# A gated-MLP layer behind a state-space convolution: where the output weights are queued, the order of the first loads, the order of four f tiles, and the second pair's first weights

## The chip, the cores and the metric

The kernel runs on one core of a Trainium2 chip. The core has a matrix engine (TensorE, PE in the profile, with its weight loads as PEld), a vector engine (VectorE, DVE), a scalar engine (ScalarE, ACT), GpSimd (POOL), and SyncE (SP), which here only issues transfers. Sixteen DMA engines move data between the device memory and the on-chip memory; SP, ACT and POOL each have a queue of their own into them. The metric is the device time of one execution in microseconds. The median of three runs of the kernel before is 1020.4 us (1020.36 to 1022.5).

## The reference

One layer of a network, 2048 tokens of width 640, in float32. Cut to what matters:

```python
mod = (silu(c) @ w_mod).reshape(6, 640)          # sa, ca, ga, sb, cb, gb
h = layernorm(x) * (1 + ca) + sa
x = x + ga * ssm_conv(h)                         # long convolution, by transforms over 2048 tokens
h = layernorm(x) * (1 + cb) + sb
gate = h @ w1; up = h @ w3                       # [2048, 640] @ [640, 1728]
out = x + gb * ((silu(gate) * up) @ w2)          # [2048, 1728] @ [1728, 640]
```

## The kernel before

The first 427 us compute the modulation and the convolution up to its last inverse transform and leave the transformed rows in `zs` in device memory. The change lies in what follows, the second layer norm and the gated MLP.

**Tiling.** The 2048 tokens are four quarters of 512, taken in two pairs: quarters A and B of pair 0, then of pair 1. The 1728 columns of w1 and w3 are cut into 14 f tiles of 128 (`NFT`); the last one, 13, holds the 64 remaining columns of both. float32 operands are split into a rounded high part and a low part (`split`, L1025: ACT copies the high part `gh` or `uh`, DVE subtracts to get the low part `gl` or `ul`), and a product is three matmuls, high x high, high x low, low x high (`prod3`, L1046).

**Stages of a pair.** First the quarters' input: a tile of 128 tokens gets its `zs` rows (`x_get`, L941: five transfers of z and one of x on SP's queue), its last transform on PE, the addition and the statistics on DVE, the root on POOL (`x_mid`, L950), the normalization on ACT (`x_norm`, L965), and is then turned by transposes on PE (`turn_a`, `turn_b`). Pair 0 has its first four tiles from before (`x_first`, L913); the next four are done between the first f tiles. For pair 1 all of it is done between the output steps of pair 0 (`prepare`, L1255, a table of step numbers).

Then the f tiles. Some are done plainly (`plain`, L1058: quarter A or B alone, 15 matmuls for the gate and 15 for the up part): 0, 13, 1 and 2 in pair 0, 13 alone in pair 1. The others go through `seven` (L1113), a Strassen-Winograd scheme over both quarters with sums of weight blocks made on POOL (`w_sums`) and split (`w_split`). Its operands `T1`, `T2`, `T4` and `T3` are sums of the turned inputs (`x_sums`, `x_sum_split`, `x_late`).

Then the outputs (`outputs`, L1173), 28 steps of 15 matmuls for a pair: 14 f tiles for quarter A, then 14 for B. Step n issues the load of the w2 tile of step n + 3 (`load`), has POOL multiply that of n + 2 by gb (`gate`), has ACT and DVE split that of n + 1 together with h (`operands`), runs `side(n)`, and then the matmuls. At the end of a quarter DVE adds the accumulators to x, and `tail` turns and adds the last 128 columns.

**What sets the order.** All weights share one ring of four buffers, `rw` (L1038). A scheduler orders the instructions of each engine, except where `in_order` holds: then an engine's instructions stay in the order of the program. This holds for the output stage. An engine's queue of transfers is in order too: a transfer that waits for its buffer holds all those behind it. `issue_after` puts an instruction behind another on its engine.

The lines that matter for the steps below:

```python
            load(n + 3)                                   # L1211, in the loop over output steps
            gate(n + 2)
            operands(n + 1)
            got = [x_get(4 + i, x, there, nc.scalar if i == 1 else SQ) ...]   # L1303
        for f in simple:                                  # L1318
            hB[f] = h_tile()
            plain("B", f, hB[f])
```

## Time and profile before

| | |
|---|---|
| median of three runs | 1020.4 us |
| the profiled execution | 1021.97 us |
| its span | 1020.2 us |
| mean granted clock of TensorE | 0.937 |
| HBM read, written | 108.93 MB, 31.46 MB |

| engine | busy us | share of the span | instructions |
|---|---|---|---|
| PEld | 693.6 | 68% | 8214 |
| DVE | 721.7 | 71% | 1230 |
| ACT | 542.9 | 53% | 796 |
| POOL | 346.6 | 34% | 330 |

Rows of a timeline give the start in us from the span's start, the duration in us, the engine (SPq or ACTq is an engine issuing a transfer), the line, the operation with out<-in by the program's names, the count of merged instructions, and in brackets how long the engine had been idle and what released it. L102 is a helper that records every operation of this part of the program, so groups are told apart by their tiles: `gh<-rw` is the cast of a weight's high part, `gl<-rw,gh` the subtraction for its low part, `A<-zs` a z load, `T<-...` a normalized tile or, as `T<-s`, one of the sums' splits, `ident` marks a transpose, `rw<-rw,gbr` the multiply by gb, `S<-rw` a sum of weight blocks. Matmul rows name the moving operand first. The profiled time is taken on one execution; it is 1.77 us longer than its span.

### The profile page before, as it was taken

To read this page: it belongs to the slowest core of one execution; us is meant where nothing else is said; L and a number is where in the kernel's file an instruction comes from. 1 tells how busy PE (TensorE), PEld (TensorE's weight loads), DVE (VectorE), ACT (ScalarE), POOL (GpSimd) and SP (SyncE) were. 2 spreads that over 40 slices of the span, in tenths; PEclk is the share of its full clock that TensorE was granted. 3 is DMA by queue.
4 is the path that set the end of the run, shared out by engine and by line. 5 is a ranking of instruction groups with operands and counts; after the bars stand their busy time and mean duration, and the time that the engine had idled before them with its cause. 6 is when DMAs were issued, how large, how long until landed. Compare 5 with 4: busy or idle time off the path is not lost.

```text
span 1020.2 us, 20715 instructions
## 1 busy us (share of the span) xinstructions
PE 930.7 (91%) x8214; PEld 693.6 (68%) x8214; DVE 721.7 (71%) x1230; ACT 542.9 (53%) x796; POOL 346.6 (34%) x330
## 2 busy tenths in 40 slices
PE   5998798899889888788999999999889999999998
PEld 2535454666666666566888888766668888888876
DVE  4598966888888985657566675777586666676755
ACT  3658674999999954155433332354543333333332
POOL 1543332444454611313322231544352222233441
PEclk9855787999999999798999999999889999999999
DMA  9463495465555688593311112879432111113443
GB/s 260 167 236 116 189 210 175 124 162 141 142 147 145 179 214 262 177 251 96 91 52 52 52 53 93 220 241 235 129 117 78 52 52 52 52 39 91 129 158 126
DMA packets 104004, 141.73 MB, mean 139 GB/s; under 512 B 20612, under 2 KB 62724, under 8 KB 103908
## 3 DMA queue, kind: packets, MB, share of 16 engines
q1 hardware_dynamic: 98740, 129.66, 43.9%
q0 software_dynamic: 2304, 7.74, 2.4%
q10 hardware_dynamic: 2864, 3.02, 1.1%
q8 instruction: 64, 1.05, 0.4%
q14 instruction: 32, 0.26, 0.1%
HBM read 108.93 MB, written 31.46 MB: 138 GB/s over the span
## 4 chain that ended last, share of the span: by engine, by line
PE 59%; ACT 15%; DVE 9%; DMA 8%; issue 4%; POOL 4%; SPq 1%; ACTq 0%; DVEq 0%; POOLq 0%
PE ps L102 44%; ACT cs L135 3%; ACT A L135 3%; ACT ph L135 3%; DMA A<-zs 2%; PE pa L432 2%; PE p L570 2%; ACT L135 2%; DMA zs<-zt 2%; PE pq L444 2%; DMA rw<-in_w_dram 1%; PE pt L539 1%; PE pk L521 1%; PE pu L406 1%; PE pm L299 1%
## 5 line engine op out<-in xcount | busy, mean ns | idle before, releaser
L102 DVE TENSOR_TENSOR s<-ps,s 128x512 f32<-128x512 f32 x138 | 94.7, 687 | 77.6 <-PE ps L102 77.0
L472 POOL TENSOR_TENSOR ph<-thi,iota 128x1024 int32<-128x1024 int32 x40 | 85.4, 2134 | 177.2 <-DVE A L508 80.5
L102 DVE TENSOR_TENSOR gl<-rw,gh 128x640 fp32r<-128x640 f32 x89 | 84.3, 948 | 74.7 <-ACT gh L102 73.6
L102 ACT CAST gh<-rw 128x640 fp32r<-128x640 f32 x89 | 64.6, 726 | 122.6 <-POOL rw L102 66.6
L102 POOL TENSOR_TENSOR rw<-rw,gbr 128x512 f32<-128x512 f32 x56 | 82.6, 1483 | 123.1 <-DMA rw<-in_w_dram 117.9
L102 POOL TENSOR_TENSOR S<-rw 128x256 f32<-128x256 f32 x46 | 35.4, 771 | 178.0 <-DVE S0l L102 152.5
L102 PE MATMUL ps<-xA,gh 128*128 128x512 f32 x280 | 89.7, 399 | 2.8 <-ACT gh L102 2.2
L570 PE MATMUL p<-uk,s 128*64 128x256 f32 x640 | 79.3, 390 | 13.7 <-PE pa L432 5.6
L102 PE MATMUL ps<-gh,uh 128*128 128x512 f32 x224 | 88.2, 394 | 0.0
L102 PE MATMUL ps<-gl,uh 128*128 128x512 f32 x224 | 87.8, 392 | 0.0
L102 PE MATMUL ps<-gh,ul 128*128 128x512 f32 x208 | 81.6, 392 | 0.0
L570 PEld LDWEIGHTS p<-uk,s 128*64 128x64 f32 x640 | 45.3, 139 | 39.1 <-PE pa L432 8.4
L102 PEld LDWEIGHTS ps<-xA,gh 128*128 128x128 f32 x280 | 53.4, 192 | 15.9 <-ACT gh L102 3.5
L102 PE MATMUL ps<-xA,gl 128*128 128x512 f32 x140 | 55.3, 395 | 0.1
L135 ACT ACTIVATE A<-pa 128x1024 f32<-128x1024 f32 x40 | 40.4, 1023 | 25.7 <-PE pa L432 24.3
L497 DVE TENSOR_TENSOR E<-A,cs 128x1024 f32<-128x1024 f32 x40 | 50.3, 1257 | 1.7 <-ACT A L135 1.7
L504 DVE TENSOR_TENSOR A<-A,ph 128x1024 f32<-128x1024 f32 x40 | 50.1, 1253 | 0.0
L612 PE MATMUL pz<-Y,i 64*128 64x128 f32 x640 | 44.9, 284 | 4.5 <-issue 3.1
L102 PEld LDWEIGHTS ps<-gh,uh 128*128 128x128 f32 x224 | 42.5, 190 | 9.3 <-DVE xm L102 0.4
L102 PEld LDWEIGHTS ps<-gl,uh 128*128 128x128 f32 x224 | 42.5, 190 | 9.1
L612 PEld LDWEIGHTS pz<-Y,i 64*128 64x128 f32 x640 | 38.8, 188 | 14.3 <-issue 11.3
L539 PE MATMUL pt<-s,K 128*64 128x128 f32 x640 | 47.8, 293 | 0.5 <-ACT uk L138 0.5
(241 smaller groups left out, 2376.7 us busy)
## 6 DMA issues: line engine op xcount, KB each, us to landing
rw<-in_w_dram SPq DMA_DIRECT2D x52, 320.0 KB
rw<-in_wg_dram SPq DMA_DIRECT2D x33, 320.0 KB
us<-u SPq DMA_DIRECT2D x16, 640.0 KB
s<-in_s_dram SPq DMA_DIRECT2D x40, 256.0 KB
i<-in_i_dram SPq DMA_DIRECT2D x40, 256.0 KB
rw<-in_wu_dram SPq DMA_DIRECT2D x29, 320.0 KB
uk<-us SPq DMA_DIRECT2D x32, 256.0 KB
zs<-zt SPq DMA_DIRECT2D x32, 256.0 KB
```

The source lines that it names most:

```text
L102: ins = fn(*args, **kw)
L135: return tc.keep_in_program_order(S.activation(*args, **kw))
L299: PE.matmul(pm[g, :n], scb[:, k], w[:, k, :], start=(k < 4), stop=(k > 0), tile_position=(0, g.start))
L406: PE.matmul(pu[h][hh * 64:hh * 64 + 64, q, :320], s1r[r], x[r, hh * 320:hh * 320 + 320], start=not (one and h == 0), stop=True, tile_posit ...
L432: keep(PE.matmul(pA[s][:, rr, :], w[r, ch, :], r2[r, js, :].rearrange("p j b -> p (j b)"), start=st, stop=not st, tile_position=(r.start, 0)))
L444: keep(PE.matmul(pQ[s][:, rr, :256], w[r, ch, :], rv, start=(i == 0), stop=(i == 3), tile_position=(r.start, 0)))
L472: hold(G.tensor_tensor(p, bc(thi[:, sl], 2, NPH), bc(iota, 1, SD), op=OP.mult))
L497: keep(V.tensor_tensor(EC[s][:, :, 1:3, :], AA[s][:, :, 1:3, :], mid(cs[s]), op=OP.mult))
L504: keep(V.tensor_tensor(A[:, :, 1:3, :], A[:, :, 1:3, :], mid(ph[s]), op=OP.mult))
L539: keep(PE.matmul(pt[c * 64:c * 64 + 64, g, :], kk[:, g, :], s1[:, c, :], start=True, stop=True, tile_position=(0, c * 64)))
L570: keep(PE.matmul(p2[par * 64:par * 64 + 64, pi, c, :], s2[:, pi * 2 + par, c * 64:c * 64 + 64], uk[:, 0:kn + 1:kn, f, :], start=True, stop ...
L612: ins = keep(PE.matmul(pz[:, par, (g % 2) * 2 + pi, :], i1[r, pi, c, :], Y[r, pi, c, :], start=(c == 0), stop=(c == 1), tile_position=(par ...
```

## The change

Four things, all in the MLP part.

1. In `outputs`, the w2 loads of the loop go to ACT's queue instead of SP's (`load(n + 3, S)`), and stand behind `operands(n + 1)`. The first three loads of a pair stay on SP's.
2. At the start of pair 0, SP's transfers are kept in program order (`sp_order`), all z loads go on SP's queue, and the weights of f tiles 13 and 1 stand between them. The split of f tile 0's weights is traced ahead of `x_first`, that of 13 is held behind the last turned input. POOL's stores of x to `xs` are held behind the power of `x_first`.
3. The plain f tiles of quarter B run backwards (2, 1, 13, 0), and the split weights of the last tile of quarter A are used for the first of quarter B without a new load; in pair 1 this is f tile 13.
4. The first weights of pair 1 (13, then 0) are loaded at output steps 25 and 26 of pair 0 (`fetch`, `ahead`). The last `tail` of pair 0 runs after pair 1's plain tiles. In `prepare`, a step does normalizations first, then loads, turns, and `x_mid` last.

```diff
-        for i, n in enumerate((2, 5, 8, 9, 14, 15, 16, 17)):
+        mids = (6, 8, 11, 12, 17, 18, 19, 20)
+        for i, n in enumerate(mids):
+            at(n + 2, lambda i=i: x_norm(4 * q0 + i, got[i], tiles[i // 4]))
+        for i, n in enumerate((2, 5, 8, 9, 14, 15, 16, 17)):
...
+        for i, n in enumerate(mids):
+            at(n, lambda i=i: x_mid(4 * q0 + i, got[i], g))
+        at(25, lambda: fetch(NFT - 1, "wg"))
+        at(26, lambda: [fetch(0, n) for n in ("wg", "wu")])
...
-            load(n + 3)
+            operands(n + 1)
+            load(n + 3, S)
             gate(n + 2)
-            operands(n + 1)
...
+        side(n_all)
+        in_order[0] = False
+        yield
         for t in late:
             t()
-        side(n_all)
-        in_order[0] = False
...
-            got = [x_get(4 + i, x, there, nc.scalar if i == 1 else SQ) for i, (x, there) in enumerate(rooms)]
+            sp_order[0] = True
+            got = [x_get(4, x5[0], True)]
+            fetch(last_f, "wg")
+            got.append(x_get(5, x5[1], True))
+            fetch(1, "wg")
+            fetch(1, "wu")
+            got += [x_get(6, x_place("T40")), x_get(7, x_place("T20"))]
+            sp_order[0] = False
...
+            ws = ws or plain_weights(f, ends if pair == 0 and n == 1 else None)
+            end = plain("A", f, hA[f], ws, pair == 0)
+            if n < len(simple) - 1:
+                ws = None
...
-        for f in simple:
+        for n, f in enumerate(simple[::-1]):
             hB[f] = h_tile()
-            plain("B", f, hB[f])
+            ws = ws or plain_weights(f)
+            plain("B", f, hB[f], ws)
+            ws = None
```

On SP's queue, at the start of pair 0 (behind the convolution's last store of z), the rows of the difference; `A<-zs` is a z load, `T<-in_x` a load of x:

```order
-L102 DMA A<-zs 64x4x128 x10
-L102 DMA T_5417<-in_x_dram 128x640
-L102 DMA A<-zs 64x4x128 x5
-L102 DMA T_5418<-in_x_dram 128x640
+L102 DMA A<-zs 64x4x128 x5
+L102 DMA rw<-in_wg_dram 128x640
+L102 DMA A<-zs 64x4x128 x5
+L102 DMA rw<-in_wg_dram 128x640
+L102 DMA rw<-in_wu_dram 128x640
+L102 DMA A<-zs 64x4x128 x5
+L102 DMA T_5443<-in_x_dram 128x640
```

The three weights (13, then both of 1) stood behind all z loads and now stand behind five and ten of them; five z loads came over from ACT.

On ACT, between the casts of f tile 0's weights and the second x tiles, before:

```order
L102 CAST gh<-rw 128x640
L102 DMA A<-zs 64x4x128 x5
L102 CAST uh<-rw 128x640
L102 ACTIVATE T_5359<-xm,rs_5308 128x640
L102 ACTIVATE T_5363<-xm,rs_5308 128x640
```

and now, up to the first Silu behind the table load:

```order
L102 CAST gh<-rw 128x640
L102 CAST uh<-rw 128x640
L102 ACTIVATE T_5367<-xm,rs_5316 128x640
L102 ACTIVATE T_5371<-xm,rs_5316 128x640
L102 ACTIVATE xA_5381<-ps,modT 128x512
L102 ACTIVATE s_5390<-ps,modT 128x512
L102 ACTIVATE xA_5401<-ps,modT 128x512
L102 CAST xA_5392<-s_5390 128x512
L102 ACTIVATE s_5410<-ps,modT 128x512
L102 ACTIVATE xA_5421<-ps,modT 128x512
L102 CAST xA_5412<-s_5410 128x512
L102 CAST gh<-rw 128x640
```

The five issues are gone from between the two casts. The row that follows the last one is `CAST uh<-rw`, for f tile 1, and then the table load.

In the output stage of pair 0, on SP around output steps 15 to 18, before:

```order
L102 DMA out_dram<-xm 128x640 x4
L102 DMA rw<-in_w_dram 128x640
L102 DMA A<-zs 64x4x128 x5
L102 DMA xm<-in_x_dram 128x640
L102 DMA rw<-in_w_dram 128x640
L102 DMA A<-zs 64x4x128 x5
L102 DMA xm<-in_x_dram 128x640
L102 DMA rw<-in_w_dram 128x640
```

and on ACT at the same place now:

```order
L102 CAST gh<-rw 128x640
L102 CAST uh<-h 128x512
L102 DMA rw<-in_w_dram 128x640
L102 ACTIVATE s_7736<-ps,modT 128x512
L102 CAST xA_7738<-s_7736 128x512
L102 ACTIVATE s_7746<-ps,modT 128x512
L102 CAST xA_7748<-s_7746 128x512
L102 CAST gh<-rw 128x640
L102 CAST uh<-h 128x512
L102 DMA rw<-in_w_dram 128x640
```

The w2 loads stood on SP between the z and x loads and now stand on ACT behind the two casts of each step; SP keeps the z, x, xs and out transfers.

## Prediction before the run

> **What bounds the kernel now.** I read the page first, then the timeline of TensorE (PE) by the idle time in brackets, then the windows for the granted clock, and last the timelines of the engines named in the brackets.
>
> ```profile
> span 1020.2 us, 20715 instructions
> ...
> PE 930.7 (91%) x8214; PEld 693.6 (68%) x8214; DVE 721.7 (71%) x1230; ACT 542.9 (53%) x796; POOL 346.6 (34%) x330
> ...
> PEclk9855787999999999798999999999889999999999
> ...
> L102 DVE TENSOR_TENSOR gl<-rw,gh 128x640 fp32r<-128x640 f32 x89 | 84.3, 948 | 74.7 <-ACT gh L102 73.6
> ```
>
> PE is busy 91% of the span and bounds the kernel; of 40 slices three near the end of the convolution and the start of the two matrix stages fall under full clock; the last row, DVE's split of a weight (0.95 us on average), is used further down. The change touches nothing before about 427 us, so only PE's gaps behind that count:
>
> ```profile
> 434.71 2.45 PE L102 MATMUL ps<-ident,T 128*128 128x128 f32 x20 [2.37 <-ACT T L102]
> ...
> 444.84 1.52 PE L102 MATMUL ps<-A,i 64*32 64x256 f32 x32
> 448.55 0.73 PE L102 MATMUL ps<-xA,gh 128*128 128x512 f32 x2 [2.19 <-ACT gh L102]
> ...
> 463.96 0.33 PE L102 MATMUL ps<-ident,T 128*128 128x128 f32 x1 [2.62 <-ACT T L102]
> 466.01 2.18 PE L102 MATMUL ps<-ident,T 128*128 128x128 f32 x9 [1.71 <-ACT T L102]
> ...
> 677.21 0.47 PE L102 MATMUL ps<-uh,gh 128*128 128x512 f32 x1 [2.12 <-DVE xm L102]
> ...
> 705.66 0.87 PE L102 MATMUL ps<-A,i 64*32 64x384 f32 x14 [1.12 <-DVE xm L102]
> ...
> 722.54 1.33 PE L102 MATMUL ps<-ident,T 128*128 128x128 f32 x5 [4.63 <-ACT T L102]
> ...
> 740.41 0.51 PE L102 MATMUL ps<-uh,gl 128*128 128x512 f32 x1 [0.56 <-DVE gl L102]
> 742.08 0.50 PE L102 MATMUL ps<-ul,gh 128*128 128x512 f32 x1 [1.17 <-DVE ul L102]
> ...
> 752.40 1.22 PE L102 MATMUL ps<-xB,gh 128*128 128x512 f32 x2 [3.15 <-ACT gh L102]
> ```
>
> The columns are start, duration, line, operation, and in brackets the idle time before it with its releaser. They fall in three groups: the start of the first pair (2.37 + 2.19 + 2.62 + 1.71 = 8.89 us), the outputs of the first pair (2.12 + 1.12 + 4.63 + 0.56 + 1.17 = 9.60), and the start of the second pair (3.15). Three of them also cost clock. The windows give, after the bounds, the time, then busy time of PE, weight loads, DVE, ACT and POOL, then granted clock, DMA share and GB/s:
>
> ```profile
> 429.00:449.00 20.00, 14.86 (x99) 10.91 (x97) 9.15 (x21) 8.14 (x12) 3.19 (x6) 1.00 1.10 287
> ...
> 466.00:472.00 6.00, 5.99 (x19) 5.14 (x20) 4.32 (x6) 4.81 (x8) 1.28 (x1) 0.52 0.23 62
> ...
> 722.00:728.00 6.00, 5.46 (x16) 4.56 (x17) 3.80 (x4) 4.21 (x7) 1.30 (x1) 0.52 0.92 312
> ...
> 752.00:759.00 7.00, 6.58 (x16) 4.72 (x17) 4.97 (x12) 3.31 (x8) 0.00 (x0) 0.54 0.72 253
> 766.00:950.00 184.00, 184.00 (x814) 152.35 (x813) 122.18 (x191) 68.35 (x127) 51.73 (x57) 1.00 0.21 62
> ```
>
> Behind 466, 722 and 752 the clock is 0.52, 0.52 and 0.54; PE's busy time there loses 5.99 x 0.48 = 2.9, 5.46 x 0.48 = 2.6 and 6.58 x 0.46 = 3.0 us. From 766 to 950 PE is busy in all 184 us at full clock, 814 matmuls of 0.226 us each, and the second pair's outputs show no gap either: there nothing can be won, only lost. At most 8.9 + 9.6 + 3.2 + 8.5 = 30 us are there to be had.
>
> **Part 1: the first loads.** Three edits act here: five z loads leave ACT's queue for SP's, SP's list is pinned with the weights of f tiles 13 and 1 between the z loads, and POOL's four stores to xs come behind the power.
>
> ```profile
> 427.31 9.66 SPq L102 DMA_DIRECT2D A<-zs  x10
> ...
> 442.18 1.29 SPq L102 DMA_DIRECT2D rw<-in_wg_dram  x2
> ```
>
> ```profile
> 427.67 4.33 ACTq L654 DMA_DIRECT2D A<-zs  x5
> 432.04 0.73 ACT L102 CAST uh<-rw 128x640 fp32r<-128x640 f32 x1 [8.45 <-DMA A<-zs]
> 433.73 1.73 ACT L102 ACTIVATE T<-xm,rs 128x640 f32<-128x640 f32 x2 [0.97 <-DVE rs L102]
> ...
> 447.78 0.72 ACT L102 CAST gh<-rw 128x640 fp32r<-128x640 f32 x1 [7.30 <-DMA rw<-in_wg_dram]
> 448.52 1.28 ACT L102 ACT_TABLE_LOAD   x1
> 449.81 0.60 ACT L102 ACTIVATE s<-ps 128x512 f32<-128x512 f32 x1
> ...
> 465.03 0.92 ACT L102 ACTIVATE T<-T,nb,rs 128x640 f32<-128x640 f32 x1 [1.12 <-DVE nb L102]
> ```
>
> ```profile
> 429.97 0.42 DVE L102 BATCH_NORM_AGGREGATE mv<-st 128x2 f32<-128x30 f32 x2
> ...
> 450.44 0.69 DVE L102 TENSOR_TENSOR h<-ps,s 128x512 f32<-128x512 f32 x1 [1.08 <-ACT s L102]
> ```
>
> Before, ACT issued for 4.33 us and so cast uh at 432.04; DVE's ul stood behind that, and the normalization behind ul, at 433.73. Without the issues uh and ul are done while the statistics still run (they end at 429.97 + 0.42 = 430.4). POOL's add of 0.20 us and power of 1.05 us, no longer split by stores, then end at 431.8, and the normalization starts at 432.0: 1.7 us earlier. PE's transposes and f tile 0 move with it, and f tile 0 ends at 444.84 - 1.7 = 443.1.
>
> The larger piece is the next one. f tile 13's weight was issued at 442.18 and ACT had its cast at 447.78, 5.6 us later; table load, Silu and then DVE's h follow in line, h at 450.44. DVE's line from there to the last normalized tile (465.03, 14.6 us after h) is what holds PE until 466.01, and the changed kernel keeps that line nearly instruction for instruction. So the term is how far h moves. In the new list of SP ten z loads and three weights stand up to the last weight that ACT needs ahead of its table load. SP needed 9.66 us for ten z loads beside ACT's five; alone I put the fifteen over the same 9.66, so 0.64 each, and with 0.65 for a weight (1.29 for two) the list is out at 427.3 + 6.4 + 1.9 = 435.7. With the 5.6 us from issue to cast that the saturated DMA (share 1.10 from 429 to 449) gave before, its cast starts at 441.3, table load and Silu end at 443.9, and f tile 0's end at 443.1 plus Silu and issue allows 443.85. Thus h at 443.9 instead of 450.4: **6.5 us**. Bounds: if the weight lands only when everything has landed (449 by the window), h is at 451.5 and the term is -1; if the clock also stays up, 6.5 + 2.9 = 9.4.
>
> In the changed kernel PE is free for the transposes at 443.1 + 13.2 (two x_mid groups of 1.52, and 15 and 30 matmuls of f tiles 13 and 1, 3.4 and 6.8) = 456.3 and waits till 443.9 + 15.5 = 459.4, so about 3.1 us idle remain. The gap of 3.15 at 752.40 was enough to lower the clock, the gaps of 2.37 and 2.19 were not; I take the nearer one and count no clock here. [...]
>
> Running f tile 2 first for the second quarter spares a second load and split of its weights: work of ACT and DVE under a full PE, counted as nothing.
>
> **Part 2: output weights on ACT's queue.**
>
> ```profile
> 689.70 0.38 SPq L102 DMA_DIRECT2D rw<-in_w_dram  x1
> ...
> 694.14 0.38 SPq L102 DMA_DIRECT2D rw<-in_w_dram  x1
> 695.49 3.27 SPq L102 DMA_DIRECT2D A<-zs  x5
> ```
>
> ```profile
> 695.55 1.29 POOL L102 TENSOR_TENSOR rw<-rw,gbr 128x512 f32<-128x512 f32 x1 [5.23 <-DMA rw<-in_w_dram]
> ...
> 701.69 1.29 POOL L102 TENSOR_TENSOR rw<-rw,gbr 128x512 f32<-128x512 f32 x1 [3.47 <-DMA rw<-in_w_dram]
> ```
>
> ```profile
> 718.00:720.00 2.00, 0.00 (x0) 0.00 (x0) 2.00 (x1) 0.00 (x0) 2.00 (x2) 1.00 0.00 0
> ```
>
> The weights issued at 689.70 and 694.14 reached POOL's multiply at 695.55 and 701.69, 5.9 and 7.6 us later, each behind five z loads on the same queue. POOL's wait delays ACT's cast, DVE's split, then the x_mid work queued behind it, and in the end the normalized tile for which PE stops 4.63 us at 722.54; the DMA engines move nothing by then (the window from 718 to 720), so it is a chain of latencies. With the weight on ACT's own queue, issued behind uh of the tile after next, POOL gets it in time. From the last x_mid group at 705.66 to the transposes at 722.54 were 16.9 us; less the 5.9 us by which the weights ran late that is 11.0, and PE, with 15 matmuls or 3.4 us an iteration and 0.9 for x_mid, arrives after three iterations, 11.1 us. I count 5.5 of the 1.12 + 4.63, nothing of 2.12 (DVE's own line), nothing of 0.56 + 1.17 (POOL's x_sums, in the same order), and the clock's 2.6: **8.1 us**. Bounds 0 and 10.2 (with the 2.12). Cost: some 50 issues on ACT of 0.38 (SP's row) to 0.87 us (ACT's five z loads in 4.33). Two casts and an issue take 0.73 + 0.73 + 0.87 = 2.3 us of 3.4, so the issue is hidden by ACT's idle time; behind it stand normalizations and the next casts. Without that cover it would be 50 x 0.38 to 0.87 = 19 to 44 us. The wait for a free buffer is none: the buffer's last reader is DVE's split two iterations back.
>
> [...]
>
> **Part 3: the second pair's start.** f tile 13's weight is loaded ahead and serves both quarters.
>
> ```profile
> 745.67 1.89 POOL L102 TENSOR_TENSOR S<-rw 128x256 f32<-128x256 f32 x2
> ```
>
> ```profile
> 749.18 3.26 DVE L102 TENSOR_TENSOR xm<-ps,xm 128x512 f32<-128x512 f32 x8
> ...
> 757.27 0.42 DVE L102 TENSOR_TENSOR S1l<-S,S1h 128x256 fp32r<-128x256 f32 x1
> ```
>
> The 3.15 us at 752.40 are the wait for a second copy of that weight, cast by ACT just before; this load and cast no longer exist, and with them goes the clock's 3.0. POOL's weight sums, 745.67 before, find their weights loaded ahead and move up. Late next is DVE. PE, with the 30 matmuls of f tile 13's two quarters from 745.5 on and four transposes, asks for S1l at 752.9. DVE's line from its eight additions (749.18) to the end of S1l (757.7) took 8.5 us; the four of the additions that are 128 wide and not 512 (by size a quarter, 0.8) and an h (0.7) move behind S1l, which leaves 7.0 and 756.2. So S1l is 0 (if its line starts 3.3 us earlier, with POOL) to 3.3 us late; I take the middle, 1.6. 3.15 + 3.0 - 1.6 = **4.5 us**; bounds 0 (DVE's line decides all) and 6.2.
>
> **Sum.** 6.5 + 8.1 + 4.5 = 19.1. Where PE follows closer on DVE's splits I expect one more pair of small waits like those at 740.41 and 742.08, 1.7 us: 17.4. The profiled execution took 1021.97, which is 1.77 more than its span; it would become 1004.6. It lies 1.6 above the median of the runs, 1020.4, so the median becomes **1003.0**.
>
> **Rivals.**
> 1. Weights on ACT's queue land no earlier, since the DMA engines are shared: part 2 gives 0, 1020.4 - 9.3 = 1011.1. For it: a DMA share over 1 while the z loads run. Against: 5.9 and 7.6 us for a weight behind z loads, and idle DMA engines at the 4.63. [...]
> 2. The pinned list is too slow: ten z loads and three weights ahead of the Silu, part 1 gives about 0: 1009.5. For it: DMA saturated from 429 to 449, in which time 20 z loads, weights and stores must all pass.
> 3. The clock stays up at the first transposes and the 2.12 goes too: 1003.0 - 2.9 - 2.1 = 998.0.
> 4. Slower: a weight is now asked for only when ACT reaches its turn, not when its buffer is free. From issue to first use PE has three iterations (10.2 us) less the two casts ahead of the issue, multiply, cast and split (1.46 + 1.29 + 0.73 + 0.95 = 4.4): 5.8 us. With a landing of 7.6 (the row at 701.69) each third iteration of 28 stops PE 1.8 us, 17 us in all, and part 2's gain is gone: 1011.1 + 17 = 1028. It decides from a landing of 5.8 us on ACT's own queue.
> 5. It doesn't do what it says: each gap is refilled by the next wait in DVE's line, 1020.
>
> **How the numbers follow.** Forecast 0.52 (its own range 999 to 1007), rival 1 0.14, rival 2 0.12, rival 3 0.11, rival 4 0.06, rival 5 0.05. The range of 995 to 1013 takes in the forecast and rivals 1 to 3 and leaves out rivals 4 and 5 and some of the spread. A measurement of this kernel tells about 0.2%, 2 us, from no change: faster 0.89, same 0.05, slower 0.06.
>
> **What would show it.** Right: normalization at 432 and h near 444; no gap over 1 us before f tile 13 of the first quarter; POOL's multiplies waiting under 2 us for a weight from 685 on; no gap over 1.5 us before the twenty-third iteration's transposes; the second quarter of f tile 13 straight behind the first. Wrong: ACT idle before uh for a weight till 445 or later (part 1), weights on ACT's queue landing over 5.8 us after issue (part 2), S1l late by over 3 us (part 3), or any new gap between 766 and 950.

## The result, and the profile after

| | before | changed |
|---|---|---|
| median | 1021.3 us (1020.4 to 1022.5) | 1006.9 us (1004.7 to 1010.8) |
| ratio | | 0.9862, 95% interval 0.9826 to 0.9899 |
| span of the profiled execution | 1020.2 us | 1003.6 us |
| mean granted clock | 0.937 | 0.946 |

The change saves 14.4 us, 1.4% (1.0 to 1.7%); 17.4 were predicted. The medians here are of four runs each; the prediction had three of the kernel before. From the page of the changed kernel, the rows that answer to those of before:

```profile
span 1003.6 us, 20635 instructions
...
PE 924.1 (92%) x8214; PEld 688.5 (69%) x8214; DVE 710.4 (71%) x1227; ACT 541.5 (54%) x793; POOL 343.0 (34%) x330
...
PEclk9856777999999999799999999999999999999999
...
L102 DVE TENSOR_TENSOR gl<-rw,gh 128x640 fp32r<-128x640 f32 x87 | 83.4, 959 | 74.1 <-ACT gh L102 73.6
```

The three slices at 8 in the row of the clock before (the 19th, 29th and 30th) are at 9 now. PE's timeline, every idle time over 0.45 us from 419 on (start, duration, line, operation, idle time before it and its releaser):

```profile
419.03 4.18 PE L102 MATMUL ps<-idle 128*128 128x512 f32 x9 [0.98 <-DVE xm L697]
...
430.20 0.77 PE L102 MATMUL ps<-ident,T 128*128 128x128 f32 x5 [0.67 <-ACT T L102]
...
448.78 1.53 PE L102 MATMUL ps<-A,i 64*32 64x384 f32 x14 [1.68 <-DMA A<-zs]
...
469.80 0.50 PE L102 MATMUL ps<-xB,gh 128*128 128x512 f32 x1 [0.49 <-ACT xB L102]
...
656.26 0.50 PE L102 MATMUL ps<-uh,gh 128*128 128x512 f32 x1 [1.02 <-DVE uh L102]
...
661.73 0.87 PE L102 MATMUL ps<-A,i 64*32 64x384 f32 x14 [2.37 <-DVE xm L102]
...
672.17 0.47 PE L102 MATMUL ps<-uh,gh 128*128 128x512 f32 x1 [2.54 <-DVE xm L102]
...
677.32 0.77 PE L102 MATMUL ps<-ident,T 128*128 128x128 f32 x5 [0.73 <-ACT T L102]
...
701.48 0.87 PE L102 MATMUL ps<-A,i 64*32 64x384 f32 x14 [1.02 <-DMA A<-zs]
...
713.63 0.76 PE L102 MATMUL ps<-ident,T 128*128 128x128 f32 x5 [0.51 <-ACT T L102]
...
730.10 0.50 PE L102 MATMUL ps<-uh,gl 128*128 128x512 f32 x1 [1.61 <-DVE gl L102]
...
731.24 0.50 PE L102 MATMUL ps<-ul,gh 128*128 128x512 f32 x1 [0.64 <-DVE ul L102]
...
745.32 0.50 PE L102 MATMUL ps<-T,S1l 128*128 128x512 f32 x1 [1.51 <-DVE S1l L102]
```

The first row is PE's first idle matmul, which fills PE's time while the last convolution rows land. It is no part of the change, and before it stood 3.03 us later:

```profile
422.06 1.19 PE L102 MATMUL ps<-idle 128*128 128x512 f32 x2 [0.98 <-DVE xm L697]
```

So 3.0 of the 16.6 us between the two spans arose ahead of the change, as executions differ, and everything behind is compared from this row on. Then the bracketed idle times read as follows. In the start of the first pair 2.37 + 0.58 + 2.19 + 2.62 + 1.71 = 9.47 became 0.67 + 1.68 + 0.49 and two below 0.45, 3.4 in all. The 1.68 is new: x_mid waits for z rows (`A<-zs`), which now stand behind the three weights in SP's list. All eleven profiles with the new loads wait 1.6 to 3.2 us in front of x_mid there, the three with the old loads (two of before, and e2 below) not at all, and in ten of the eleven half clock follows. In the first pair's outputs the gap of 4.63 became 0.51, but **new ones stand earlier, 1.02 and 2.37 at 656 and 662**; 2.54 is the old 2.12. At the second pair's start 3.15 became 1.51. The windows of the changed kernel (bounds, time, busy time of PE, weight loads, DVE, ACT and POOL, then granted clock, DMA share, GB/s):

```profile
429.00:449.00 20.00, 17.01 (x125) 11.62 (x130) 13.30 (x27) 11.06 (x16) 4.99 (x10) 0.99 1.09 266
448.00:452.00 4.00, 3.22 (x18) 1.73 (x19) 3.13 (x9) 2.35 (x3) 1.48 (x3) 0.59 1.03 400
...
732.00:736.00 4.00, 4.00 (x12) 3.10 (x11) 3.35 (x4) 2.50 (x6) 2.71 (x2) 0.57 0.08 31
766.00:945.00 179.00, 179.00 (x792) 148.20 (x791) 114.27 (x181) 66.73 (x123) 49.05 (x55) 1.00 0.23 65
905.00:999.00 94.00, 93.93 (x419) 77.30 (x417) 52.18 (x72) 34.34 (x56) 33.15 (x25) 1.00 0.38 116
```

PE still loses clock twice, near 450 and 733, for half as long each time (3.41 us for 6.83), and is full from 766 on. From the first idle matmul on the execution divides into five stages, read from the start times of PE's rows: **S**, to the first matmul with S1l; then the seven-product f tiles of the first pair (110.84 us in thirteen of the fourteen profiles of this study, 110.87 in e2); **O**, from the last S1l matmul there to the third of the second pair (so that all waits of its start fall into O); then the second pair's (135.32 in all); and **E**, from its last S1l matmul to the last matmul.

| stage | before | changed | difference |
|---|---|---|---|
| S, start of the first pair | 81.25 | 74.88 | -6.37 |
| O, outputs, second pair's start | 158.97 | 155.03 | -3.94 |
| E, outputs of the second pair | 106.74 | 103.82 | -2.92 |

The prediction had 6.5, 10.9 (8.1 + 4.5 - 1.7) and 0. In this pair of profiles S is as forecast, O gave little over a third, and E was not foreseen at all.

### The profile page after: what moved, and what is told of

It is laid out like the page before. It is cut to its first block, busy times and chain, and to the rows that moved or that the text cites. A ratio compares the mean times of both kernels' runs of the same rounds, so it can differ in the third digit from the quotient of the medians.

```text
span 1003.6 us, 20635 instructions
## 1 busy us (share of the span) xinstructions
PE 924.1 (92%) x8214; PEld 688.5 (69%) x8214; DVE 710.4 (71%) x1227; ACT 541.5 (54%) x793; POOL 343.0 (34%) x330
## 4 chain that ended last, share of the span: by engine, by line
PE 59%; ACT 16%; DVE 10%; DMA 7%; issue 3%; POOL 3%; SPq 1%; ACTq 0%; DVEq 0%; POOLq 0%
PE ps L102 44%; ACT cs L135 4%; DMA A<-zs 3%; ACT A L135 3%; ACT ph L135 3%; PE p L570 2%; ACT L135 2%; PE pa L432 2%; PE pq L444 2%; DMA zs<-zt 2%; PE pu L406 2%; PE pm L299 1%; DMA rw<-in_w_dram 1%; PE pk L521 1%; PE pt L539 1%
## 5 line engine op out<-in xcount | busy, mean ns | idle before, releaser
L102 POOL TENSOR_TENSOR rw<-rw,gbr 128x512 f32<-128x512 f32 x56 | 77.1, 1380 | 147.5 <-DMA rw<-in_w_dram 108.6
L102 PEld LDWEIGHTS ps<-xA,gh 128*128 128x128 f32 x280 | 52.7, 190 | 14.4 <-ACT T L102 1.2
L135 ACT ACTIVATE A<-pa 128x1024 f32<-128x1024 f32 x40 | 40.5, 1024 | 24.9 <-PE pa L432 23.6
```

The lines of the kernel that those rows point to most:

```text
L102: ins = fn(*args, **kw)
L135: return tc.keep_in_program_order(S.activation(*args, **kw))
```

## The experiments

Each kernel was timed in five rounds against the kernel before on the same chip, whose median there was 1022.75 us for the first four (e), 1022.25 for the next four (f) and 1021.42 for the last four (g). Stages are of each one's profiled execution. Parts 1 to 3 are those of the prediction: the first loads, the output weights, the second pair's start.

| kernel | median us | ratio to before (95%) | S | O | E |
|---|---|---|---|---|---|
| before again (g4) | 1021.69 | 1.0008 (0.9988 to 1.0028) | 80.41 | 161.66 | 106.73 |
| changed again (f1) | 1010.1 | 0.9873 (0.9836 to 0.9911) | 73.66 | 154.91 | 104.57 |
| w2 back on SP (e1) | 1014.36 | 0.9927 (0.9903 to 0.9952) | 75.65 | 158.66 | 106.52 |
| old first loads (e2) | 1015.67 | 0.9935 (0.9908 to 0.9961) | 79.79 | 157.77 | 104.52 |
| old second pair's start (e3) | 1010.52 | 0.9903 (0.9866 to 0.9940) | 74.50 | 155.09 | 104.02 |
| w2 asked one step earlier (e4) | 1007.71 | 0.9872 (0.9833 to 0.9910) | 74.43 | 156.07 | 103.85 |
| gate late, POOL adds (f2) | 1012.09 | 0.9901 (0.9880 to 0.9923) | 77.17 | 156.13 | 104.27 |
| f tiles forward (f3) | 1008.47 | 0.9869 (0.9845 to 0.9894) | 78.79 | 154.74 | 104.38 |
| x_mid first (f4) | 1008.18 | 0.9874 (0.9852 to 0.9897) | 77.55 | 155.65 | 104.75 |
| gate late, DVE adds (g1) | 1011.29 | 0.9908 (0.9882 to 0.9934) | 76.04 | 153.05 | 103.80 |
| w2 on SP, stores later (g2) | 1011.95 | 0.9904 (0.9878 to 0.9931) | 76.96 | 159.62 | 104.72 |
| only f13 ahead (g3) | 1008.40 | 0.9881 (0.9846 to 0.9915) | 76.32 | 155.86 | 103.91 |

**Output weights back on SP's queue (e1).**

```diff
-            operands(n + 1)
-            load(n + 3, S)
-            gate(n + 2)
+            load(n + 3)
+            gate(n + 2)
+            operands(n + 1)
```

> The changed kernel with the output weights of the loop back on SP's queue, ahead of gate and operands, as before the change; all else stays. Theory P (the prediction's term): worth 8.1 us, all of it in the first pair's outputs, so about 1015. Theory Q (read from the two traces): in the first pair's outputs the weights on ACT's queue land as late as behind the z loads (9 to 12 us from 644 to 690), new gaps of 2.37 and 2.54 us stand for the old 2.12 and 4.63, so there the part is worth only the clock's 2.6; the second pair's outputs, where the prediction saw nothing, give 3.3 (from the 948.79 row to the end). About 1010 to 1013, with a gap of 1 us or more near the x loads of the second pair's outputs.

1014.36 us, ratio 0.9927 against 0.9862 and 0.9873 with the change whole: part 2 is worth 5.5 to 6.6 us. That is Theory Q's 2.6 + 3.3 and not Theory P's 8.1; the median lies near P's 1015, but in this set the kernel before took 1022.75 us too. By stages 3.6 of it are in O (158.66 for 155.03) and 2.7 in E (106.52 for 103.82), as Theory Q divides it. The gap before the transposes is back at 4.62, the second pair's weights are late again; SP's and POOL's timelines of this run there:

```profile
962.68 2.03 SPq L102 DMA_DIRECT2D out_dram<-xm  x4
964.80 2.10 SPq L102 DMA_DIRECT2D rw<-in_w_dram  x3
```

```profile
968.86 6.08 POOL L102 TENSOR_TENSOR rw<-rw,gbr 128x512 f32<-128x512 f32 x4 [11.97 <-DMA rw<-in_w_dram]
```

Four stores of results stand in SP's list until DVE has made the results, and three weights stand behind them; POOL waits 11.97 us, then multiplies four weights in a row. The kernel before has the same in its own profile, POOL's wait and PE's gap behind it:

```profile
976.40 4.48 POOL L102 TENSOR_TENSOR rw<-rw,gbr 128x512 f32<-128x512 f32 x3 [11.80 <-DMA rw<-in_w_dram]
```

```profile
981.49 0.50 PE L102 MATMUL ps<-ul,gh 128*128 128x512 f32 x1 [1.18 <-DVE ul L102]
```

The 9 to 12 us for a weight on ACT's queue in Theory Q (and in e4's below) are too long: f tile 13's weight is loaded in two halves, and the pairing of issues and multiplications has to count them as one. So paired, the weights issued between 644 and 690 reach POOL 3.0 to 8.5 us later.

**The stores later, weights still on SP (g2).** On top of e1, for the second pair, the transposes of the first quarter's last columns stay and the stores move (cut; the loop over `late` now runs what is due at step n):

```diff
-                late.append(rest_of)
+                late.append((n + 1, lambda q=q, ob=ob, x=xr: tail(q, ob, x)))
+                late.append((n + (4 if last else 1), lambda q=q, x=xr: [x_out(4 * q + i, x[i]) for i in range(4)]))
```

> The run with the output weights on SP's queue once more, with one move: in the second pair's outputs the four stores of the first quarter's results stand three weights later in SP's list. Theory H: the weights were late there because SP, which issues in order, stood at the stores until their data were there, with three weights behind them (POOL waits 11.97 us for one); with the stores later the last stage falls from 106.5 to 104.3 us, as on ACT's queue, and POOL's longest wait for a weight there falls under 5 us. Theory D (the transfers themselves compete on the DMA engines, whichever queue issues them): the last stage stays at 106.5.

E fell to 104.72. The wait of 11.97 us is gone, and from 920 us on POOL's longest for a weight is 3.88; two of 10.3 and 10.9 us at the very start of the stage are in e1 and before alike, and PE doesn't stop behind them:

```profile
950.34 5.52 POOL L102 TENSOR_TENSOR rw<-rw,gbr 128x512 f32<-128x512 f32 x3 [3.88 <-DMA rw<-in_w_dram]
...
966.23 1.29 POOL L102 TENSOR_TENSOR rw<-rw,gbr 128x512 f32<-128x512 f32 x1 [3.83 <-DVE ul L102]
```

Theory H: in E the gain of the new queue is that a store which waits for its data no longer holds the weights up. Most of it, 1.8 us of E, is had as well by moving three weights past the stores. By the ratios g2 is 2.3 us faster than e1, and the two intervals overlap, so the stage carries this reading.

**The first loads as before (e2).** Its diff is part 1 taken back, all of its edits together, but for the backward order (cut):

```diff
...
-            sp_order[0] = True
-            got = [x_get(4, x5[0], True)]
-            fetch(last_f, "wg")
...
+            rooms = [(x5[0], True), (x5[1], True), (x_place("T40"), False), (x_place("T20"), False)]
+            got = [x_get(4 + i, x, there, nc.scalar if i == 1 else SQ) for i, (x, there) in enumerate(rooms)]
...
```

> The changed kernel with the first loads as before: five z loads on ACT's queue, no fixed order on SP, the weights of f tiles 13 and 1 asked for in their turn, f tile 0's weight split traced behind the normalization, POOL's stores not held behind the power. The second quarter still runs backwards. Theory P: slower by 6.5 us, 1013.4. Theory Q (the traces from the first idle matmul to the first S1l matmul differ by 6.4 us): the same, 1013.3, and of it 6.0 are idle time of PE and 1.2 the clock. Rival R: the backward order of the second quarter, which stays here, carries a part of it; then the loss is 5 us or less.

1015.67 us, 0.9935: 6.3 to 7.5 us slower than the change whole. S is 79.79, 4.9 more than the changed kernel's first profile. Theory P holds for the time; the stage alone would be Rival R's. How part 1's worth divides between the five z loads, the order on SP and POOL's stores isn't shown.

**The same order of f tiles for both quarters (f3).**

```diff
-            if n < len(simple) - 1:
+            if n < len(simple) - 1 or pair == 0:
...
-        for n, f in enumerate(simple[::-1]):
+        for n, f in enumerate(simple):
```

> The changed kernel with the plain f tiles of the first pair in the same order for both quarters, so that f tile 2's weight isn't used twice running and f tile 0's comes first again. Theory P: costs nothing, 1007. Theory R (from the run with the old first loads, which kept the backward order and lost 4.9 of the 6.4 us of that stage): the backward order is worth the other 1.5 us, 1008.5, with a wait for a weight or its split at the start of the second quarter.

0.9869, the changed kernel's own ratio: in the time the backward order shows nothing (Theory P). S is 78.79, above all ten profiles with the new loads and the backward order (73.66 to 77.55), with a wait of 1.59 us at the start of the second quarter; one profile. It isn't settled whether 1 to 3 us are there.

**x_mid ahead of the transposes (f4).**

```diff
+        for i, n in enumerate((2, 5, 8, 9, 14, 15, 16, 17)):
+            at(n, lambda i=i: got.__setitem__(i, x_get(4 * q0 + i, x_tile())))
         for i, n in enumerate(mids):
+            at(n, lambda i=i: x_mid(4 * q0 + i, got[i], g))
             at(n + 2, lambda i=i: x_norm(4 * q0 + i, got[i], tiles[i // 4]))
...
-        for i, n in enumerate((2, 5, 8, 9, 14, 15, 16, 17)):
-            at(n, lambda i=i: got.__setitem__(i, x_get(4 * q0 + i, x_tile())))
...
-        for i, n in enumerate(mids):
-            at(n, lambda i=i: x_mid(4 * q0 + i, got[i], g))
```

> The changed kernel with x_mid back in its old place in an iteration, ahead of the transposes, and the normalization's order as before. Theory P: in no term, costs nothing, 1007. Rival: where x_mid waits for its z load at the head of PE's queue it holds the transposes back; from iterations 15 to 17, which have both, 1 to 2 us slower, 1008 to 1009.

0.9874, O 155.65: no worth of x_mid's place in an iteration is seen.

**The second pair's start as before (e3)** has no weight fetched ahead, f tile 13's weight twice, the tail in its old place.

```diff
-        at(25, lambda: fetch(NFT - 1, "wg"))
-        at(26, lambda: [fetch(0, n) for n in ("wg", "wu")])
...
+        for t in late:
+            t()
         side(n_all)
         in_order[0] = False
-        yield
-        for t in late:
-            t()
...
-            if n < len(simple) - 1:
+            if n < len(simple) - 1 or pair == 1:
...
-        next(output)
-    next(output, None)
+        next(output, None)
```

> The changed kernel without the second pair's early start: no weight fetched ahead, f tile 13's weight loaded, cast and split a second time for the second quarter, the last tail of the first pair's outputs back in its old place. The order of x_mid behind the turns stays as changed. Theory P: slower by 4.5 us, 1011.4, with a gap near 3 us and half clock before f tile 13's second quarter. Theory Q (gaps and clock of the two traces from 730 on: 0.56 + 1.17 + 3.15 + 3.0 before, 1.61 + 0.64 + 1.51 + 0.37 + 1.7 after): slower by 2 us, 1009.

0.9903, interval 0.9866 to 0.9940: 3 to 4 us slower than the change by the ratios, not told apart from it by the intervals. O is 155.09, the same as with the change. The gap is back in full; PE's timeline and the windows around it:

```profile
743.03 0.72 PE L102 MATMUL ps<-xB,gh 128*128 128x512 f32 x2 [3.16 <-ACT gh L102]
```

```profile
736.00:739.00 3.00, 3.00 (x17) 2.54 (x15) 2.62 (x3) 0.73 (x2) 3.00 (x4) 1.00 0.36 109
739.00:743.00 4.00, 0.87 (x4) 0.38 (x2) 4.00 (x10) 1.27 (x3) 2.62 (x3) 1.00 0.00 0
743.00:747.00 4.00, 2.55 (x9) 1.51 (x10) 2.92 (x6) 2.32 (x6) 0.00 (x0) 1.00 0.85 328
```

PE is idle for 3.16 us, as at 752.40 in the kernel before, but **the clock stays at 1.00**. The price of 3.0 us that the prediction gave this gap does not belong to the gap alone. What this part is worth without it is the difference of the idle times there, 0.56 + 1.18 + 3.16 + 1.22 = 6.1 to 1.61 + 0.64 + 1.51 + 0.37 = 4.1: 2 us. In the changed kernel's profile half clock from 732.01 to 735.42 takes 1.7 of these back.

**Only f tile 13's weight ahead (g3).**

```diff
-        at(26, lambda: [fetch(0, n) for n in ("wg", "wu")])
```

> The changed kernel with only f tile 13's weight fetched ahead for the second pair; f tile 0's two weights are asked for in their turn, so that POOL's sums of them come later. Theory S: the waits of 1.61 and 0.64 us before the end of the first pair's outputs are DVE's splits stretched beside those sums on POOL; they fall back to the 0.56 and 1.17 of before, and S1l comes later by 2 us or more: gap before it 3 to 5 us in place of 1.5. The stage 1 to 3 us longer. Rival: the sums aren't what stretches them; 1.61 and 0.64 stay.

Nothing moved: 1.61, 0.64 and 1.47 in PE's timeline, and POOL makes the sums at the same place (731.57, right behind x_sums' first subtraction). Without the call f tile 0's weights are asked for just as early, so the test did not bear on Theory S. In e3 the sums start 5.3 us behind the first of the two waits (736.31 for 731.04), with the change 2.6 us ahead of it (727.50 for 730.10), and there the waits are 0.56 and 1.18. That speaks for Theory S; no run moves the sums alone.

**The weights asked for one step earlier (e4).**

```diff
-        for n in range(3):
+        for n in range(4):
             load(n)
...
-            load(n + 3, S)
+            load(n + 4, S)
```

> The changed kernel with the output weights asked for one iteration earlier (n + 4 in place of n + 3, still on ACT's queue behind the casts; four buffers as before, four loads ahead of the loop). Theory Q: the weights land late because ACT asks for them only 10.2 - 4.4 = 5.8 us ahead of their use, and they take 9 to 12 us while z loads run; 3.4 us more slack removes most of POOL's waits for a weight between 650 and 690 and the gaps 1.02, 2.37, 2.54 and 1.02 that follow from them: 3 to 6 us faster, 1001 to 1004. Rival B: the DMA engines are saturated there (share 1.0 to 1.13), what comes earlier for one comes later for another, and x_mid then waits for its z loads: 1006 to 1008.

0.9872, O 156.07: no gain, Rival B's number. Yet the gap of 2.37 before x_mid did go, as Theory Q said; in its place came 0.83 and 1.64 further on. What holds PE there isn't one late weight alone.

**The gate behind the accumulation (f2, g1).** POOL's 56 multiplications go; DVE multiplies the four accumulators of a quarter by the gate where it added x, and x is added behind that, by POOL in f2 (DVE in the last quarter), by DVE in g1. The diff of f2, cut:

```diff
-            gate(n + 2)
...
-                V.tensor_tensor(xr[k][:, :512], acc[k], xr[k][:, :512], op=OP.add)
+                og = room(k) if last else h_tile()
+                V.tensor_tensor(og, acc[k], gbr, op=OP.mult)
+                (V if c and last else G).tensor_tensor(xr[k][:, :512], xr[k][:, :512], og, op=OP.add)
```

> The changed kernel with the 56 multiplications of the output weights by the gate taken from POOL; instead DVE multiplies the four accumulators of a quarter by the gate where it added them to x, and POOL (DVE in the last quarter) adds x behind that. The product is the same up to rounding. Theory S: DVE's split takes 1.78 us beside POOL's multiplication and 0.68 without, and a weight passes POOL for 1.3 us ahead of its cast; both go. The gap of 2.54 us at the quarter's boundary (DVE's additions begin 2.2 us late behind two stretched instructions) falls under 1 us, and the gap of 2.37 before it goes: 4 to 7 us faster than the changed kernel, about 1000 to 1003. Theory B: the z loads' landing is what holds the outputs up; then the two gaps stay and the time is within 2 us of the changed kernel's, 1005 to 1009.

> As the run with the gate behind the accumulation, but x is added by DVE, in the turn of the quarter's last additions, so that POOL has neither the 56 multiplications nor the 16 additions. Theory S (a tensor operation of POOL stretches DVE's operation beside it, gl from 0.83 to 1.63, ul from 0.68 to 1.77): the gaps of 2.49 before the transposes and 5.23 before S1l, which stood behind POOL's four additions, go back to 0.7 and 1.5, and the outputs keep the 4 us or less of idle time up to the second quarter's end: 2 to 5 us faster than the changed kernel in the same stage (152 to 153 for 155 us), time 1003 to 1006. Theory B (DVE's own line is full there, its four more additions a quarter cost what POOL's did): the stage stays at 155 to 156, time 1007 to 1010.

f2 took 1012.09 us, g1 1011.29: neither beats the changed kernel. But the timelines show why the freed POOL time didn't help. POOL's and DVE's in f2 at the quarter's boundary, and what PE waited:

```profile
671.26 6.07 POOL L102 TENSOR_TENSOR xm<-xm,h 128x512 f32<-128x512 f32 x4 [1.12 <-DVE h L102]
```

```profile
672.88 1.63 DVE L102 TENSOR_TENSOR gl<-rw,gh 128x640 fp32r<-128x640 f32 x1
674.44 1.77 DVE L102 TENSOR_TENSOR ul<-h,uh 128x512 fp32r<-128x512 f32 x1
676.14 1.22 DVE L102 SCALAR_TENSOR_TENSOR nb<-mv,rs 128x1 f32<-128x1 f32 x1
```

```profile
678.36 0.76 PE L102 MATMUL ps<-ident,T 128*128 128x128 f32 x5 [2.49 <-ACT T L102]
...
748.22 0.79 PE L102 MATMUL ps<-T,S1l 128*128 128x512 f32 x1 [5.23 <-DVE S1l L102]
```

And DVE's same three operations in g1, with POOL idle:

```profile
672.30 0.80 DVE L102 TENSOR_TENSOR gl<-rw,gh 128x640 fp32r<-128x640 f32 x1
673.03 0.67 DVE L102 TENSOR_TENSOR ul<-h,uh 128x512 fp32r<-128x512 f32 x1
673.63 0.14 DVE L102 SCALAR_TENSOR_TENSOR nb<-mv,rs 128x1 f32<-128x1 f32 x1
```

Beside POOL's additions they take 1.63, 1.77 and 1.22 us, without them 0.80, 0.67 and 0.14. PE's gap of 2.49 in f2 follows from it and is gone in g1. Ahead of the 5.23 two splits of T and one of a weight take 3.13 and 1.88 us beside POOL, in g1 1.27 and 0.82; there the gap is 3.23, for an h behind DVE's own additions. From 640 to the end of the second quarter's x_mid and transposes g1 has 3.2 us of idle PE, the changed kernel 8.2 and 5.1 in its two profiles. O in g1 is 153.05, at Theory S's 152 to 153, yet the time says 1011. One profiled execution is no better here than about 2 us, and a gain of g1 isn't shown.

**Both kernels again (f1, g4).**

> The changed kernel once more, beside the runs of this call, for how much the time and the stages of a profiled execution vary of themselves. Both theories: 1005 to 1009. Stages of its first profile: 74.9 us from the first idle matmul to the first S1l matmul, 155.0 us from the first pair's last S1l matmul to the third of the second pair, 103.8 us from the last S1l matmul to the last matmul. Theory P (the clock's loss belongs to a gap): the same gaps cost the same half clock again. Theory G (the clock is set on a fixed grid of 3.41 us, by the idle share of the stretch before): the same gaps cost half clock or not as they fall on the grid, and the middle stage varies by 1.5 to 3 us.

> The kernel before once more, for a second profile of its stages: 81.3 us from the first idle matmul to the first S1l matmul, 159.0 from the first pair's last S1l matmul to the third of the second pair, 106.7 from the last S1l matmul to the end. Theory G (clock on a fixed grid): the gap of 3.15 us before f tile 13's second quarter is there again, but it lowers the clock only if it leaves more than about 1.8 us idle in one stretch of 3.41 us of the grid; it may pass without. Theory P: it costs half clock for 6.8 us again.

The changed kernel's times are 1006.9 in one set and 1010.1 in another, at ratios of 0.9862 and 0.9873: the medians of the two sets differ by 3.2 us, the ratios by 0.0011. Its stage S had half clock for 3.41 us the first time and none the second, though the second execution had the larger gap (2.1 us for 1.68): 74.88 and 73.66. A gap of 2.30 us ahead of x_mid brought 6.83 us of half clock in f1 where 2.37 brought none in the first profile, as Theory G has it, yet O came out the same (154.91 for 155.03), since other waits were shorter. The kernel before again had 6.83 us of half clock at f tile 13's second quarter, Theory P's number. Theory G's limit of 1.8 us fails there: the gap of 3.16 us left 1.92 us idle in one stretch of the grid, which full clock followed, and 1.67 in the next (with a wait of 0.42 behind it), which half clock followed.

## Why the prediction was right in sum and wrong in its parts

**Part 1, the first loads: right in the mechanism, 6.5 forecast, 5.1 by the stages.** Over the ten profiles with the new loads and the backward order S is 75.7 on average, the two of before 80.8: 5.1 us; by the time of e2 6.3 to 7.5. The mechanism is as told. Rows of the changed kernel, of ACT and of SP, and DVE's h:

```profile
429.22 1.74 ACT L102 ACTIVATE T<-xm,rs 128x640 f32<-128x640 f32 x2 [7.90 <-DVE rs L102]
...
439.92 0.73 ACT L102 CAST uh<-rw 128x640 fp32r<-128x640 f32 x1 [3.32 <-DMA rw<-in_wu_dram]
440.66 1.28 ACT L102 ACT_TABLE_LOAD   x1
441.95 0.60 ACT L102 ACTIVATE s<-ps 128x512 f32<-128x512 f32 x1
```

```profile
424.28 3.28 SPq L102 DMA_DIRECT2D A<-zs  x5
...
434.24 0.54 SPq L102 DMA_DIRECT2D rw<-in_wu_dram  x1
```

```profile
442.59 0.69 DVE L102 TENSOR_TENSOR h<-ps,s 128x512 f32<-128x512 f32 x1 [1.08 <-ACT s L102]
```

From the idle matmul the normalization starts after 10.2 us (429.22 - 419.03) for 11.7 before, 1.5 earlier for 1.7 forecast, and h after 23.6 for 28.4, 4.8 earlier for 6.5. The weight that decides took 5.7 us from issue (434.24) to cast (439.92), 5.6 forecast. The mis-sized term is SP's list: ten z loads and three weights took 10.5 us (424.28 to 434.78) where I had 8.4, from "alone I put the fifteen over the same 9.66". The 3.1 us of idle time that the sum left before the transposes came earlier, as x_mid's wait for z rows, and with half clock in most profiles.

**Part 2, the output weights: the sign right, the place wrong.** 8.1 us were put down to the first pair. It gave about 3.4 there by the stages (O is 158.66 and 159.62 with the weights on SP, 155.7 on average in the seven profiles with them on ACT's queue and the second pair's start of the change) and 2.5 in the second pair (106.7 and 106.5 to 104.2). Three steps failed.

First, "POOL gets it in time". ACT's issues and POOL's multiplications of the changed kernel, for the pair's 5th, 20th and 22nd weight, paired in order:

```profile
618.19 0.36 ACTq L102 DMA_DIRECT2D rw<-in_w_dram  x1
...
681.66 0.35 ACTq L102 DMA_DIRECT2D rw<-in_w_dram  x1
...
691.15 0.34 ACTq L102 DMA_DIRECT2D rw<-in_w_dram  x1
```

```profile
621.20 1.29 POOL L102 TENSOR_TENSOR rw<-rw,gbr 128x512 f32<-128x512 f32 x1 [2.45 <-DMA rw<-in_w_dram]
...
688.31 1.30 POOL L102 TENSOR_TENSOR rw<-rw,gbr 128x512 f32<-128x512 f32 x1 [6.30 <-DMA rw<-in_w_dram]
...
698.59 1.30 POOL L102 TENSOR_TENSOR rw<-rw,gbr 128x512 f32<-128x512 f32 x1 [1.49 <-DMA rw<-in_w_dram]
```

A weight is on its way for 3.0 us while no z loads run, and 6.7 and 7.4 us while they do, beyond the 5.8 of rival 4. ACT asks later than SP did, since it comes to the issue only behind the casts, and the x_mid that stands behind such a weight in DVE's line is the new gap of 2.37. The sign "POOL's multiplies waiting under 2 us for a weight from 685 on" failed at 688.31 with 6.30. Rival 4 was right about the landing and wrong about the price: e4 gave the slack back and won nothing, as other waits of DVE's line took its place. POOL's multiplications stretched operations of DVE in that line, as its additions did in f2: in the changed kernel DVE's split of h at 668.50 stands beside two of them and took 1.78 us, at 663.95 without them 0.68. So the other queue brought no earlier landing: beside the z loads a weight takes 6.7 and 7.4 us on ACT's queue, and took 5.9 and 7.6 on SP's. What SP's waiting in order cost is another matter: 1.8 us of this kernel's E (106.52 in e1, 104.72 in g2).

Second, the clock's 2.6 (and 3.0 in part 3). O had half clock for 13.7 us in both profiles of before and 7.3 on average in the seven of the change, 3.2 us of work for 5.6 forecast: the gap before the transposes went, but two short waits (1.61 + 0.64) now lower the clock at 732 in the changed kernel's first profile; in f3 the same two do not.

Third, "the second pair's outputs show no gap". They had 1.18 at 981.49, eleven matmuls that began 0.31 to 0.45 us after the one before them where 0.23 is usual (two in the changed kernel's first profile), and POOL without a weight for 11.80 us: I looked at the stretch from 766 to 950 and stopped.

**Part 3, the second pair's start: 4.5 forecast, 0 to 2 by the stages.** By the ratios it is 3 to 4, which the intervals don't tell from nothing. The 3.15 went, S1l came 1.51 late for 1.6 forecast. What failed is the clock's 3.0, as e3 shows, and that POOL's sums "move up" at no cost: beside them the subtraction ahead of the two splits takes 1.21 us for 0.69, the splits 1.34 and 1.22 for 0.82 and 1.76, so that 0.56 + 1.17 became 1.61 + 0.64. That is 0.5 us more, and now near enough together to cost clock; the 1.7 that the sum took off for one more pair of small waits was about right in size, for another reason.

**The sum.** 5.1 + 4.6 + 2.5 = 12.2 by the stages' averages, 12.2 and 14.4 by the medians. The forecast's 17.4 is too high by 3 to 5 us, and it came that near in part by luck: O was overrated by 6.3 and S by 1.4, and E, which the sum put at nothing, gave 2.5 back. No new gap arose between 766 and 950, nothing came near rival 4's 1028, and of rival 1 the landing "no earlier" came true, its price of nothing for part 2 did not.

## What to carry to other kernels

A load that has nothing to wait for should not stand in an in-order queue behind a store that waits for a result (POOL waited 11.97 us for such a weight in e1); moving it to another engine's queue does that (E 106.52 to 103.82), and so does moving the store (104.72). When a wait on a chain of four engines is removed, price the gain by what is next in line on the engine that carries the chain, here DVE, and count half clock as a chance, not as a property of the gap (behind 3.15 us of idle time it lasted 6.83 us before, behind 3.16 in e3 there was none). Look at the whole timeline of the second round of a loop too, also where PE seems full.

## What the runs showed of the hardware

**The granted clock.** In the clock's records of the two profiles, before and changed, every change of the granted clock lies a whole multiple of 3.413 us from every other of the same profile. These points don't go with the kernel: one lies 5.33 us behind the first idle matmul before (427.39 - 422.06), and 5.78 us behind it in the changed kernel (424.81 - 419.03). Between 428 and 1000 half clock lasted 6.83 us from 464.93, 720.93 and 751.65 before, and 3.41 us from 448.71 and 732.01 in the changed kernel. Worked out from PE's rows, in stretches of 3.41 us between such points: idle time of PE in the stretch ahead of each half clock, and in the two most idle stretches that full clock followed.

| profile | ahead of half clock (start) | ahead of full clock (start) |
|---|---|---|
| before | 3.08 (461.52), 3.03 (717.52), 2.40 (748.24) | 1.88 (430.80), 1.50 (444.45) |
| changed | 1.84 (445.29), 2.13 (728.60) | 1.60 (670.57), 1.51 (742.25) |

Half clock followed 1.84 and not 1.88, so the idle time of one stretch doesn't decide alone here, and what else does isn't known. The 3.15 us before f tile 13's second quarter fell 2.40 into one stretch and 0.75 into the next and were followed by 6.83 us at half clock, and 1.61 and 0.64, together 2.13 in one stretch, by 3.41 us. In e3 the clock stayed at 1.00 from 736 to 747, over the gap of 3.16. Stage S goes with the dips: 73.7 us with none (one profile), 74.4 to 75.7 with one of 3.41 (four), 76.0 to 77.6 with 6.83 (five).

**DVE beside POOL's tensor operations.** In the kernel before, behind 428 us, the fifteen splits of h (`ul<-h,uh`, 512 wide) with no POOL operation beside them took 0.68 to 0.69 us; of the twelve that stood beside POOL's multiplications of weights alone, nine took 1.76 to 1.79 and three 0.68. In the changed kernel it was 0.68 to 0.69 for the 22 without POOL, and two of the five beside multiplications took 1.78. Beside POOL's additions in f2 it was 1.77, in g1 without them 0.67 (rows above). DVE's operations on the accumulators were not stretched: its additions of them to x (`xm<-ps,xm`, 512 wide) took 0.67 to 0.69 us without POOL and 0.67 to 0.68 beside it in the kernel before (nine and seven), and its four products with the gate took 2.47 us in f2, where POOL began at 671.26 in the middle of them, and 2.46 in g1.
